# Pooled attention with a mixture-of-depths block: v loaded by parity of heads, keys outermost, and a new order of all operations

## The chip, the cores and the metric

The kernel runs on one core of a Trainium2 chip. The metric is the device time of one execution in microseconds, as the median of several runs. TensorE, VectorE, ScalarE, GpSimd and SyncE run side by side, each its own list of instructions in order; SyncE (SP) issues nearly all transfers, and a core's transfers are carried by 16 DMA engines.

## The reference

q, k and v have the shape (8, 8, 576, 64): batches, heads, positions, width, all float32. k and v are averaged over windows of 8 positions, so each head has 72 pooled keys.

```python
k_p = k.reshape(B, H, Sp, pool, D).mean(axis=3)
v_p = v.reshape(B, H, Sp, pool, D).mean(axis=3)
scores = scale * np.matmul(q, k_p.transpose(0, 1, 3, 2))
attn = softmax(scores)                       # over the 72 pooled keys
x = (attn @ v_p).transpose(0, 2, 1, 3).reshape(B, S, 512)
scores = np.einsum('bsd,d->bs', x, w_gate)   # one number for each row
top_idx = the 128 rows of the batch with the highest score
h = np.maximum(x[top_idx] @ w1, 0.0); ye = h @ w2      # 512 -> 1024 -> 512
out = x;  out[top_idx] = x[top_idx] + sigmoid(scores[top_idx]) * ye
```

## The kernel before

The eight batches go through one pipeline. For each batch `front` declares: fold k over its windows (`pool_k`, L413 and L414), transpose and finish it (`k_trans`, L419 to L428), transpose q in two halves (`q_trans`, L435), scores in two halves on TensorE (L450, L456) with the exponentials on ScalarE (L467), fold v (`pool_v`, L479 to L511), centre its gate column (`centre`), five chunks of attention (`attend`, L550 and L557, division L575 and L579, a store of the rows to `out`), and `rank`, which finds the 128 best rows, gathers them by an indirect DMA and computes their gate. Batches 0 to 3 then go through `dense` one by one (up L731, down L740, scatter L715). Batches 4 and 5, and 6 and 7, go through `pair`, which replaces the eight block products of two batches by seven (`seven`, L824 and L841).

The 72 keys of a head are split into 64 (K0) and 8 left over (K1). The tile VR holds v for one batch, 128 partitions by 5 blocks of 512 numbers (one window of 8 positions by 64 wide, 2 KB). Partitions 0 to 63 belong to even heads, 64 to 127 to odd ones; block 1 + m has the 64 keys of the head pair m, block 0 the leftover keys of all four heads of that parity on 32 partitions. `load_v2` fills the large blocks and `load_v1` the leftover one. There are two tiles VR, one for even and one for odd batches, and only one tile KR for k. KD is the part of the pooled keys that multiplies the leftover scores, masked by `block`; `diag` is the mask that places leftover values of the right head into VP. Both masks come from the number of the partition, by small integer instructions in `opening` (L325 to L330).

Nothing is scheduled when the program is built: every operation is added to a `Plan` with a number, and `ORDER`, a list of all 832 numbers written out in the kernel, is the order in which they are emitted, and so the order within each engine and within SP's queue. `BANKS` gives the PSUM bank of each product that may choose. Operations `heat` (L307) and `fill` (L313) are products of zeros that keep TensorE running. All loads of a batch and all stores are issued by SP from one line (L291), in that order; an issue that has to wait for a buffer or a result holds up all issues behind it.

Of the kernel before, what the change touches and what calls it, by code (L numbers as in the profile page):

```python
# [11 lines left out]
OP = mybir.AluOpType  # L12
# [129 lines left out]
def direct_path(ctx, tc, q, k, v, moe_w_gate, moe_w1, moe_w2, moe_capacity, out, flag):  # L142
# [64 lines left out]
    KD = sb("kd", [128, 2, 2, NP, K1], n=2)  # L207
# [32 lines left out]
    code = sb("code", [128, 2])  # L240
# [57 lines left out]
    def opening():  # L298
# [22 lines left out]
        def grid():  # L321
            for x in VP:
                nc.vector.memset(x[:, 0 : 1 + NP, D], float(POOLW))
            nc.vector.tensor_scalar(ident, ident, 0.0, None, op0=OP.is_equal)
            nc.vector.tensor_scalar(ints[:, 1:2], ints[:, 0:1], 5, None, op0=OP.arith_shift_right)  # L325
            nc.vector.tensor_scalar(ints[:, 2:3], ints[:, 0:1], 3, None, op0=OP.arith_shift_right)
            nc.vector.tensor_scalar(ints[:, 2:3], ints[:, 2:3], 2 * NP - 1, None, op0=OP.bitwise_and)
            nc.vector.tensor_copy(code, ints[:, 1:3])
            nc.vector.tensor_scalar(block, block, code[:, 0:1], None, op0=OP.is_equal)
            nc.vector.tensor_scalar(diag, diag, code[:, 1:2], None, op0=OP.is_equal)  # L330
            nc.vector.memset(heavy[:, 0:NP], float(POOLW))
            nc.vector.tensor_scalar(heavy[:, NP : 3 * NP], diag, float(POOLW), None, op0=OP.mult)
# [54 lines left out]
    def load_v1(b):  # L387
        i = b % 2
        for p in range(2):
            load(VR[i][64 * p : 64 * p + 32, 0], bass.AP(tensor=v.tensor, offset=v.offset + b * H * S * D + p * S * D + K0 * POOLW * D,  # L390
                 ap=[[2 * S * D, NP], [POOLW * D, K1], [1, POOLW * D]]), (), [("VQ", i, p)])

    def load_v2(b):
        i = b % 2
        for m in range(NP):
            load(VR[i][:, 1 + m], bass.AP(tensor=v.tensor, offset=v.offset + b * H * S * D + 2 * m * S * D,
                 ap=[[S * D, 2], [POOLW * D, K0], [1, POOLW * D]]), (), [("VR", i, m)])

    def load_gate():
        w = moe_w_gate  # L400
        for p in range(2):
            load(WG[64 * p : 64 * p + 64, 1 : 1 + NP], bass.AP(tensor=w.tensor, offset=w.offset + p * D, ap=[[0, 64], [2 * D, NP], [1, D]]), (), [("WG", p, 0)])
            load(WG[64 * p : 64 * p + 32, 0], bass.AP(tensor=w.tensor, offset=w.offset + p * D, ap=[[2 * D, NP], [0, K1], [1, D]]), (), [("WG", p, 1)])
# [13 lines left out]
    def k_trans(b):  # L417
# [7 lines left out]
        def two():  # L425
            y = KT[b % 2].rearrange("p j s m -> p (j s) m")
            nc.vector.tensor_tensor(out=y, in0=one_, in1=two_, op=OP.add)
            nc.vector.tensor_tensor(out=KD[b % 2].rearrange("p j s i m -> p (j s) i m"),  # L428
                                    in0=y[:, :, K0:SP].rearrange("p n (one m) -> p n one m", one=1).to_broadcast([128, 4, NP, K1]),
                                    in1=block.rearrange("p (a i b) -> p a i b", a=1, b=1).to_broadcast([128, 4, NP, K1]), op=OP.mult)  # L430
# [41 lines left out]
    def pool_v(b):  # L472
        i = b % 2
        x = VR[i].rearrange("p m (w d) -> p m w d", d=D)
        raw = [("VR", i, m) for m in range(NP)] + [("VQ", i, p) for p in range(2)]
# [274 lines left out]
    def differences():  # L750
        keys = [("VRx", 0)] + [("VR", 0, m) for m in range(NP)]
# [544 lines left out]
```

## Time and profile before

| | us |
|---|---|
| median of 3 runs | 381.98 |
| lowest and highest | 381.77, 384.44 |
| the profiled execution | 382.64 |
| its span from first to last instruction | 380.9 |
| TensorE busy | 238.6 |
| VectorE busy | 171.6 |
| ScalarE busy | 110.8 |
| GpSimd busy | 37.2 |

The profile is one execution. A view of it lists groups of instructions, waits, the chain of work that ended last, or the busy time of each engine in stretches of the span. "PE" is TensorE, "DVE" VectorE, "ACT" ScalarE, "POOL" GpSimd, "SPq" the issuing of transfers by SyncE. [...] "DMA share" is the mean busy share of the 16 DMA engines: 1.0 means that all move data, 0.13 that on the average two of them do.

### The profile page before, as it was taken

What the parts mean: (1) busy time and instruction counts of PE and PEld (TensorE: products, weight loads), DVE (VectorE), ACT (ScalarE), POOL (GpSimd) and SP (SyncE); (2) the same over time, 40 slices, a digit from 0 to 9 for tenths busy, and PEclk for the clock granted to TensorE, in tenths of its full rate; (3) what the DMA queues carried; (4) which work ended last, traced back from release to release, by engine and by line L of the source; (5) the groups of instructions that cost most, each with busy time, mean ns of one, the idle gap of its engine ahead of it and who ended that gap; (6) DMA issues with size and microseconds to landing.
All of it is one profiled execution on the core that took longest, in us unless ns stands there. A gap on an engine that the chain in (4) does not pass through costs nothing.

```text
span 380.9 us, 7492 instructions
## 1 busy us (share of the span) xinstructions
PE 238.6 (63%) x3081; PEld 166.4 (44%) x3081; DVE 171.6 (45%) x380; ACT 110.8 (29%) x372; POOL 37.2 (10%) x96
## 2 busy tenths in 40 slices
PE   5402225919103979803359930977669999999990
PEld 2201113505002648501125820436645677999980
DVE  8104109452007787307045703635173636648751
ACT  1100123605004457302033301362404761641300
POOL 5000000000000040000100300002010431310031
PEclk9955655977855799975588995895859999999996
DMA  5131264712374892115559334534613344200012
GB/s 189 58 111 62 64 195 126 264 48 76 92 241 132 275 364 109 58 55 170 170 153 324 112 123 137 162 137 133 203 40 125 102 139 99 95 29 1 2 55 65
DMA packets 19858, 48.50 MB, mean 127 GB/s; under 512 B 3048, under 2 KB 4072, under 8 KB 18920
## 3 DMA queue, kind: packets, MB, share of 16 engines
q1 hardware_dynamic: 18536, 43.75, 36.1%
q0 software_dynamic: 1280, 4.20, 3.5%
q8 instruction: 26, 0.43, 0.4%
q14 instruction: 16, 0.13, 0.1%
HBM read 36.39 MB, written 11.55 MB: 126 GB/s over the span
## 4 chain that ended last, share of the span: by engine, by line
DMA 41%; PE 28%; SPq 18%; DVE 9%; issue 2%; ACT 0%; POOL 0%; DVEq 0%; POOLq 0%
DMA vr<-in_v_dram 29%; SPq L291 18%; PE pJ L740 5%; DMA kr<-in_k_dram 4%; DMA qr<-in_q_dram 3%; DMA dr<-sc 3%; PE pJ L824 3%; PE pA L550 3%; DVE vr L479 3%; PE pJ L731 2%; PE pA L824 2%; PE pA L841 2%; PE pA L557 2%; PE pJ L841 2%; PE pS L824 1%
## 5 line engine op out<-in xcount | busy, mean ns | idle before, releaser
L550 PE MATMUL pA<-vp,et 64*64 64x66 f32 x1056 | 28.0, 250 | 73.5 <-DVE xs L579 61.2
L479 DVE TENSOR_TENSOR vr<-vr 128x1280 f32<-128x1280 f32 (+1 forms) x16 | 18.5, 1157 | 115.7 <-DMA vr<-in_v_dram 115.3
L550 PEld LDWEIGHTS pA<-vp,et 64*64 64x64 f32 x1056 | 22.5, 156 | 86.1 <-DVE xs L579 64.4
L740 PE MATMUL pJ<-w,ht 128*128 128x512 f32 x64 | 36.7, 708 | 11.7 <-DMA w<-in_moe_w_dram 11.7
L731 PE MATMUL pJ<-xg,w 128*128 128x128 f32 x256 | 35.6, 298 | 0.0
L731 PEld LDWEIGHTS pJ<-xg,w 128*128 128x128 f32 x256 | 33.5, 211 | 4.4 <-issue 3.1
L450 PE MATMUL pS<-qt,kt 32*64 32x320 f32 (+1 forms) x512 | 20.7, 433 | 22.0 <-DVE qt L435 22.0
L664 ACT ACTIVATE cmp<-sr,sc 128x640 bf16<-128x640 f32 (+3 forms) x40 | 32.5, 812 | 3.7 <-DMA sr<-dr 3.1
L570 ACT ACTIVATE za<-pA,eps 128x8 f32<-128x8 f32 (+1 forms) x36 | 9.6, 266 | 76.2 <-PE pA L557 74.9
L500 ACT COPY vp<-vp 32x66 f32<-32x66 f32 x16 | 3.9, 245 | 84.0 <-DVE vp L495 83.9
L467 ACT ACTIVATE et<-pS 128x512 f32<-128x512 f32 (+1 forms) x40 | 21.9, 559 | 16.8 <-PE pS L456 16.7
L557 PE MATMUL pA<-vp,ed 64*64 64x264 f32 (+1 forms) x288 | 25.9, 422 | 0.3 <-issue 0.3
L740 PEld LDWEIGHTS pJ<-w,ht 128*128 128x128 f32 x64 | 13.3, 228 | 26.9 <-issue 13.9
L579 DVE TENSOR_TENSOR xs<-pA,rz 128x512 f32<-128x512 f32 (+1 forms) x34 | 21.9, 644 | 6.0 <-DVE rz L575 2.6
L450 PEld LDWEIGHTS pS<-qt,kt 32*64 32x64 f32 x512 | 9.8, 136 | 31.3 <-DVE qt L435 23.2
L435 DVE STREAM_TRANSPOSE qt<-qr 128x1024 f32<-128x1024 f32 (+1 forms) x16 | 21.9, 1369 | 0.9 <-DMA qr<-in_q_dram 0.8
L715 POOL DMA_INDIRECT out_dram<-y,ix x8 | 9.0, 1126 | 105.0 <-DVE rz L575 42.0
L413 DVE TENSOR_TENSOR kr<-kr 128x1152 f32<-128x1152 f32 (+1 forms) x10 | 11.1, 1110 | 14.4 <-DMA kr<-in_k_dram 14.4
L575 DVE RECIPROCAL rz<-za 128x8 f32<-128x8 f32 (+1 forms) x40 | 7.4, 185 | 19.3 <-ACT za L570 19.2
L686 POOL TENSOR_SCALAR ix<-tg 128x1 int32<-128x1 f32 x8 | 2.4, 294 | 129.5 <-DVE tg L682 129.4
L313 PE MATMUL pJ<-zero 128*128 128x256 f32 x32 | 12.8, 520 | 3.4 <-DVE zero L304 3.4
L456 PE MATMUL pS<-qt,kd 128*32 128x128 f32 (+1 forms) x256 | 12.7, 318 | 0.0
(200 smaller groups left out, 386.2 us busy)
## 6 DMA issues: line engine op xcount, KB each, us to landing
vr<-in_v_dram SPq DMA_DIRECT2D x32, 256.0 KB
out_dram<-xs SPq DMA_DIRECT2D x32, 256.0 KB
kr<-in_k_dram SPq DMA_DIRECT2D x7, 1152.0 KB
qr<-in_q_dram SPq DMA_DIRECT2D x8, 640.0 KB
qr<-in_q_dram SPq DMA_DIRECT2D x8, 512.0 KB
w<-in_moe_w_dram SPq DMA_DIRECT2D x4, 1024.0 KB
sr<-dr SPq DMA_DIRECT2D x5, 320.0 KB
kr<-in_k_dram SPq DMA_DIRECT2D x3, 384.0 KB
```

Source lines behind the costliest of these rows:

```text
L291: i = engine(eng).dma_start(out=dst, in_=src)
L435: nc.vector.transpose(out=QT[b % 2][h].rearrange("p j s (t g) -> p t (j s) g", g=G), in_=QR[b % 2][h].rearrange("p t (j s g) -> p t (j s) ...
L450: nc.tensor.matmul(pS[64 * s : 64 * s + 64, i, 0:n], KT[b % 2][p, j, s, 0:K0], q[p, j, s, 0:n], start=(j == 0), stop=(j == 1))
L467: nc.scalar.activation(o.rearrange("p n (g t) -> p n g t", g=G), pS[:, 0:m, y : y + w].rearrange("p n (t g) -> p n g t", g=G), AF.Exp, sca ...
L479: nc.vector.tensor_tensor(out=o, in0=u, in1=w, op=OP.add)
L550: nc.tensor.matmul(o[s][64 * w : 64 * w + 64, E * y : E * y + E], et[p, m, 64 * u : 64 * u + 64], VP[i][p, 1 + m, :], start=(y == 0), stop ...
L557: nc.tensor.matmul(o[s][64 * w : 64 * w + 64, 0 : n * E], ed[p, u : u + 64], VP[i][p, f : f + n, :], start=False, stop=True)
L579: nc.vector.tensor_tensor(out=XS[i][c].rearrange("p (m s d) -> p s m d", s=2, d=D)[:, k], in0=o[:, :, :, 0:D], in1=RZ[i][:, c, 0:nz].rearr ...
L664: nc.scalar.activation(cmp[0:n, 0:m], SR[r][0:n, 0:m], AF.Sign, bias=SC[i][0:n, c : c + 1], scale=-1.0, accum_out=RK[0:n, b, c])
L731: nc.tensor.matmul(acc[:, cap * f : cap * f + cap], w1[g][:, d, 128 * f : 128 * f + 128], XG[i][:, d, :], start=(d == 0), stop=(d == DB - 1))
L740: nc.tensor.matmul(job(ds)[0:cap, :], HT[i][f // 4][:, f % 4, :], w2[f // 4][:, f % 4, :], start=(f == 0), stop=(f == FB - 1))
L824: nc.tensor.matmul(bank[:, cap * f : cap * f + cap], b[:, d, 128 * f : 128 * f + 128], a[:, d, :], start=d == 0, stop=d == 1)
```

## The change

`load_v2` issues two transfers for a batch instead of four. Before, one transfer took a pair of heads: head, then key, then the 512 numbers of a window, to 128 partitions. After, one takes the heads of one parity: key, then pair, then the 512 numbers, to 64 partitions and four blocks of each. `load_v1` still issues two, but its leftover keys come ordered by key, then pair, instead of pair, then key. The leftover rows of the gate, KD, and the masks follow that order: the mask number of a partition is now its pair plus four times a bit of its 32-block, which takes five small instructions in the opening instead of three. As a batch has two operations fewer, the plan has 816 operations, and `ORDER` and `BANKS` are new.

```diff
 ORDER = [int(x) for x in """
-35 30 28 27 29 36 0 32 2 33 37 50 51 21 7 38 52 4 14 39 53 34 40 41 43 54 47 55 1 44 42 67 56 68 124 45 122 49
...
+2 10 28 35 34 27 4 26 36 49 30 31 29 48 37 32 50 0 38 39 44 41 42 47 45 46 1 43 40 51 121 119 19 8 7 22 21 52
...
-    KD = sb("kd", [128, 2, 2, NP, K1], n=2)
+    KD = sb("kd", [128, 2, 2, K1, NP], n=2)
...
-            nc.vector.tensor_scalar(ints[:, 2:3], ints[:, 0:1], 3, None, op0=OP.arith_shift_right)
-            nc.vector.tensor_scalar(ints[:, 2:3], ints[:, 2:3], 2 * NP - 1, None, op0=OP.bitwise_and)
-            nc.vector.tensor_copy(code, ints[:, 1:3])
+            nc.vector.tensor_scalar(ints[:, 2:3], ints[:, 0:1], NP - 1, None, op0=OP.bitwise_and)
+            nc.vector.tensor_scalar(ints[:, 3:4], ints[:, 1:2], 1, None, op0=OP.bitwise_and)
+            nc.vector.tensor_copy(code, ints[:, 1:4])
+            nc.vector.scalar_tensor_tensor(code[:, 1:2], code[:, 2:3], float(NP), code[:, 1:2], op0=OP.mult, op1=OP.add)
...
             load(VR[i][64 * p : 64 * p + 32, 0], bass.AP(tensor=v.tensor, offset=v.offset + b * H * S * D + p * S * D + K0 * POOLW * D,
-                 ap=[[2 * S * D, NP], [POOLW * D, K1], [1, POOLW * D]]), (), [("VQ", i, p)])
+                 ap=[[POOLW * D, K1], [2 * S * D, NP], [1, POOLW * D]]), (), [("VQ", i, p)])
 
     def load_v2(b):
         i = b % 2
-        for m in range(NP):
-            load(VR[i][:, 1 + m], bass.AP(tensor=v.tensor, offset=v.offset + b * H * S * D + 2 * m * S * D,
-                 ap=[[S * D, 2], [POOLW * D, K0], [1, POOLW * D]]), (), [("VR", i, m)])
+        for p in range(2):
+            load(VR[i][64 * p : 64 * p + 64, 1 : 1 + NP], bass.AP(tensor=v.tensor, offset=v.offset + b * H * S * D + p * S * D,
+                 ap=[[POOLW * D, K0], [2 * S * D, NP], [1, POOLW * D]]), (), [("VR", i, p)])
...
-            load(WG[64 * p : 64 * p + 32, 0], bass.AP(tensor=w.tensor, offset=w.offset + p * D, ap=[[2 * D, NP], [0, K1], [1, D]]), (), [("WG", p, 1)])
+            load(WG[64 * p : 64 * p + 32, 0], bass.AP(tensor=w.tensor, offset=w.offset + p * D, ap=[[0, K1], [2 * D, NP], [1, D]]), (), [("WG", p, 1)])
...
-            nc.vector.tensor_tensor(out=KD[b % 2].rearrange("p j s i m -> p (j s) i m"),
-                                    in0=y[:, :, K0:SP].rearrange("p n (one m) -> p n one m", one=1).to_broadcast([128, 4, NP, K1]),
-                                    in1=block.rearrange("p (a i b) -> p a i b", a=1, b=1).to_broadcast([128, 4, NP, K1]), op=OP.mult)
+            nc.vector.tensor_tensor(out=KD[b % 2].rearrange("p j s m i -> p (j s) m i"),
+                                    in0=y[:, :, K0:SP].rearrange("p n (m one) -> p n m one", one=1).to_broadcast([128, 4, K1, NP]),
+                                    in1=block.rearrange("p (a b i) -> p a b i", a=1, b=1).to_broadcast([128, 4, K1, NP]), op=OP.mult)
...
-        raw = [("VR", i, m) for m in range(NP)] + [("VQ", i, p) for p in range(2)]
+        raw = [("VR", i, p) for p in range(2)] + [("VQ", i, p) for p in range(2)]
```

## Rows read from the trace of the kernel before

**Rows 1.** The page: busy time of the engines, then the shares of the last chain by line.

```profile
PE 238.6 (63%) x3081; PEld 166.4 (44%) x3081; DVE 171.6 (45%) x380; ACT 110.8 (29%) x372; POOL 37.2 (10%) x96
...
DMA vr<-in_v_dram 29%; SPq L291 18%; PE pJ L740 5%; DMA kr<-in_k_dram 4%; DMA qr<-in_q_dram 3%; DMA dr<-sc 3%; PE pJ L824 3%; PE pA L550 3%; DVE vr L479 3%; PE pJ L731 2%; PE pA L824 2%; PE pA L841 2%; PE pA L557 2%; PE pJ L841 2%; PE pS L824 1%
```

**Rows 2.** VectorE's waits: releaser, then total us, times, longest us.

```profile
DVE vr L479 <- DMA vr<-in_v_dram: 115.3, 7, 24.8
...
DVE kr L413 <- DMA kr<-in_k_dram: 14.4, 2, 8.5
DVE vr L491 <- DMA wg<-in_moe_w_gate_dram: 9.1, 1, 9.1
```

**Rows 3.** Chain that ended last, the longest of six pieces of v: start us, us.

```profile
92.18 21.11 DMA vr<-in_v_dram
```

**Rows 4.** DMA view of 0 to 30 us in 40 slices of 0.75 us.

```profile
DMA  0077999783111111111112112111114899211111
GB/s 0 0 106 303 397 369 380 198 360 142 52 49 55 49 49 55 49 49 55 49 49 98 55 63 79 55 49 49 49 49 93 168 358 319 83 49 49 49 52 57
```

**Rows 5.** Stretches: us, busy us (instructions) of each engine, clock, DMA share, GB/s.

```profile
8.50:15.00 6.50, 4.38 (x57) 2.33 (x56) 2.08 (x4) 1.25 (x3) 0.00 (x0) 1.00 0.13 51
134.00:143.00 9.00, 6.68 (x161) 3.80 (x159) 7.81 (x15) 4.70 (x16) 3.90 (x7) 1.00 1.04 365
```

**Rows 6.** The page's transfers by group: issuer, count, KB each.

```profile
vr<-in_v_dram SPq DMA_DIRECT2D x32, 256.0 KB
```

**Rows 7.** Stretches of 4 to 275 us, columns as in rows 5.

```profile
0.00:274.90 274.90, 146.59 (x2164) 92.62 (x2164) 111.70 (x241) 75.35 (x274) 18.73 (x65) 0.75 0.47 150
13.00:274.90 261.90, 138.80 (x2107) 88.50 (x2105) 102.67 (x196) 73.33 (x272) 13.87 (x33) 0.74 0.47 150
113.40:155.90 42.50, 33.23 (x584) 23.25 (x585) 33.85 (x65) 22.83 (x87) 4.10 (x7) 0.82 0.60 204
274.90:300.00 25.10, 20.49 (x322) 11.83 (x322) 16.16 (x36) 8.18 (x30) 2.66 (x4) 0.80 0.23 70
300.00:366.00 66.00, 66.00 (x570) 57.48 (x570) 38.53 (x83) 27.29 (x69) 13.45 (x26) 1.00 0.24 70
124.00:128.00 4.00, 4.00 (x46) 2.80 (x49) 3.61 (x5) 0.75 (x6) 0.00 (x0) 0.50 0.79 266
```

**Rows 8.** SP in order of time: start, us, what it issues.

```profile
75.50 8.82 SPq L291 DMA_DIRECT2D vr<-in_v_dram  x3
...
178.19 0.54 SPq L291 DMA_DIRECT2D vr<-in_v_dram  x1
```

**Rows 9.** A group of instructions by line: busy us, mean ns of one | idle before.

```profile
L428 DVE TENSOR_TENSOR kd<-kt,block 128x128 f32<-128x128 f32 x8 | 2.3, 292 | 0.3
```

**Rows 10.** TensorE at full clock: up and down, then one chunk of attend in the chain.

```profile
302.07 4.63 PE L731 MATMUL pJ<-xg,w 128*128 128x128 f32 x40
...
311.94 3.70 PE L740 MATMUL pJ<-w,ht 128*128 128x512 f32 x8
...
306.69 0.63 PE pA L550 x32
307.32 0.45 PE pA L557 x8
```

**Rows 11.** VectorE in order of time: first q transpose, first folds of batches 0 and 7.

```profile
9.41 1.24 DVE L435 STREAM_TRANSPOSE qt<-qr 128x1024 f32<-128x1024 f32 x1
...
31.22 2.35 DVE L479 TENSOR_TENSOR vr<-vr 128x1280 f32<-128x1280 f32 x2 [20.57 <-DMA vr<-in_v_dram]
...
274.89 2.35 DVE L479 TENSOR_TENSOR vr<-vr 128x1280 f32<-128x1280 f32 x2 [10.50 <-DMA vr<-in_v_dram]
```

**Rows 12.** SP's waits up to 275 us: releaser, total us, times, longest us.

```profile
SPq L291 <- DVE xs L579: 15.2, 3, 9.1
SPq L291 <- DVE rz L575: 13.4, 5, 5.2
...
SPq L291 <- DMA dr<-sc: 10.9, 1, 10.9
```

More of the change, by code (lines that the diff above doesn't have):

```diff
@@ L239, in direct_path @@
     ints = sb("ints", [128, 6], I32)
-    code = sb("code", [128, 2])
+    code = sb("code", [128, 3])
     block = sb("block", [128, NP])
@@ L750, in differences @@
     def differences():
-        keys = [("VRx", 0)] + [("VR", 0, m) for m in range(NP)]
+        keys = [("VRx", 0)] + [("VR", 0, p) for p in range(2)]
         t1 = [(part(VR[0], 0, 2, 512), keys), (part(VR[0], 1024, 2, 512), keys), (part(QR[0][0], 0, 2, 512), [("QR", 0, 0)]),
```

63 rows, old and new, of tables (BANKS, ORDER) are left out of this document.

## The prediction

> **What bounds the kernel now.** I read the page first: no engine is busy for more than 63% of the span, yet transfers of v and SP's issuing hold nearly half of the chain that ended last (29% and 18%) [rows 1]. So the time is waiting, and the list of waits says whose: VectorE stands 115.3 us, in seven waits, before the first fold of v (L479) until a load of v has landed; 14.4 us more go on k and 9.1 us on the gate [rows 2]. In the chain six pieces "DMA vr<-in_v_dram" follow one another, the longest 21.11 us [rows 3].
>
> The DMA view of the first 30 us shows why they are so long. While k and the first half of q are in flight the core moves 303 to 397 GB/s; from about 8 us on, with only v in flight, the share is 0.1 and the rate 49 to 55 GB/s [rows 4]. Measured over 8.5 to 15 us it is a share of 0.13 at 51 GB/s; where everything flows (134 to 143 us) it is 1.04 at 365 GB/s [rows 5]. 0.13 of 16 engines is two engines, at some 25 GB/s each. The source of each large load of v has an outer dimension of 2 (the two heads of a pair), those of k and q one of 128. A load of 256 KB [rows 6] over two engines takes 262 KB / 51 GB/s = 5.1 us, four of them 20.6 us: the pieces of the chain.
>
> That is throughput, not latency. 32 such loads hold two engines for 32 x 5.1 = 164 us. Up to 274.9 us, where the last v is folded, the share is 0.47, so 129 us of all sixteen [rows 7]; 164 x 2/16 = 20.5 of it is v's, and the other loads and stores put about 109 us on every engine. The two that carry v thus have 109 + 164 = 273 us to do in 274.9 us. They are the bound of the front of the kernel; k, q, weights and stores have a share on the same two and queue behind v, and SP's issues block: three issues of v take 8.82 us, against 0.54 us for one that meets no queue [rows 8]. After 300 us TensorE is the bound, 66.0 of 66.0 us busy [rows 7].
>
> **The change, part by part.** *Large v loads:* four of 256 KB become two of 512 KB, outer dimension 64 keys on both sides, 2 KB pieces as before. No row has a load of that shape, so its rate lies between two engines (51 GB/s) and sixteen (365 GB/s) [rows 5]; the nearest row is that of loads with an outer dimension of 128, and I take sixteen: 1.05 MB in 2.9 us instead of 20.6 us. [...]
>
> *Small v loads, gate loads:* 64 KB and 8 KB, outer dimension 4 becomes 8. They are a twentieth of v's bytes; a gain of up to 1 us each, hidden behind the large ones, which land later. I count zero; uncovered it is 0 to 1 us per batch. The 9.1 us wait for the gate goes, since what it queued behind is gone.
>
> *SP:* 16 issues fewer, 16 x 0.54 = 9 us of SP's time [rows 8], counted at nothing: SP is ahead once its issues no longer block. Per batch this leaves no wait that was not there; the order decides which transfer queues behind a waiting one (rival C).
>
> *Key-first layout:* the product that fills kd (L428) still writes 128 x 128 elements, 0.29 us [rows 9]; were the inner broadcast costlier, it could double, 8 x 0.3 = 2.4 us; I take 0, as elements and operands are the same. The setup gets two more VectorE instructions on one column; each no longer than that product, 0 to 0.6 us in an opening that waits for loads, taken as 0.
>
> *New order:* what counts is where it puts work against the folds. In its SP list k, half of q, half of v and the gate come first, then the rest of q and v. In its VectorE list both transposes of q stand before the first fold. And ahead of the last batch's first fold TensorE now has four groups "up" and five "down" of batch 2 and two chunks of attend that came behind it before. At full clock these are 4 x 0.46, 5 x 0.46 and 2 x 1.08 us [rows 10], with a pick 6.5 us.
>
> **The sum.** Opening: by the shapes 3.6 MB stand up to the end of v(0), at 365 GB/s [rows 5] 10 us, after the 2 us until data flow [rows 4]. VectorE has the first q transposed at 10.7 us and needs 1.5 us for the second, which is a quarter larger [rows 11]. So the first fold comes at 13 us instead of 31.2 us [rows 11].
>
> Front: now the first folds of batch 0 and batch 7 are 274.89 - 31.22 = 243.7 us apart, 34.8 us per batch [rows 11]. What a batch costs with v at hand is seen from 113.4 to 155.9 us, from the first fold of batch 2 to the point where VectorE waits for batch 4: two batches in 42.5 us, VectorE 33.85 us or 80% busy, granted clock 0.82 [rows 7]. Seven times 21.25 us is 149 us. The other way, VectorE's work: 111.7 us before 274.9 us [rows 7], some 4 us that the order moves ahead (an estimate: a difference of weights, a one-hot and divisions), less 10.5 us before the first fold (9.0 us up to 13 us today [rows 7] and the second transpose), is 105 us; at 80% 132 us. I take the middle, 141 us: the stretch began with a cold TensorE (clock 0.50 up to 128 us [rows 7]), which a front without long waits doesn't have, but it needed a DMA share of only 0.60. The new front needs 129 us of share in 154 us, 0.84, which the engines reach where they are fed [rows 5]; TensorE's 146.6 us there [rows 7] fit even at today's clock. So VectorE with its hand-overs is what is late next.
>
> Tail: 380.9 - 274.9 = 106 us, less the 6.5 us moved ahead = 99.5 us.
>
> 13 + 141 + 99.5 = 253.5 us of span; the profiled execution's 382.64 us stands 1.7 us over its span of 380.9 us and 0.7 us over the median: **255 us**.
>
> **Rivals.** *A, the forecast:* v spread over sixteen engines, the front at VectorE's pace: 246 to 263 us (132 and 149 us for the front), with some 4 us to either side 242 to 267 us.
>
> *B, v lands at half rate and the transfers stay the bound.* Each new load writes 64 partitions instead of 128. If such a load moves at half of 365 GB/s while it holds the queue, v keeps all engines 5.8 us per batch instead of 2.9, and the front's demand rises from 129 to 152 us; at a share of 0.9 that takes 169 us up to the last fold, at 0.84 it takes 181 us, where the sum has 13 + 141 = 154 us: 255 + 15 to 255 + 27, 270 to 282 us. For it: no row shows such a load. Against it: it decides only if the share stays under 152/154, and the order can spread the load. [...]
>
> *C, other waits of SP's in-order queue come on the path.* In front of 275 us SP waits also for divisions (xs 15.2, rz 13.4 us) and for dr (10.9 us) [rows 12]. Whatever load stands behind such a wait is late too. If these 40 us stay and nothing hides them: 255 + 40 = 295 us; half of it 275. Against it: the waits are long because the divisions wait for v themselves.
>
> *D, better than the stretch:* VectorE at 90% in the front, 117 us: 231 us; with the tail's cold part (0.80 up to 300 us [rows 7]) warm as well some 3 us less. So 231 to 242 us. Against it: the best long stretch has 80%.
>
> *E, no spread, slower.* If the shape does not set the number of engines, v stays at 51 GB/s. Then the new VectorE list hurts: the folds of batch 1 stand ahead of the shift that batch 0's attend needs, so two batches of v, 41 us of two engines, come before the first attend, as now, and every later load is issued in an order made for quick v. Today's 382 us, plus up to one load of 20 us: 385 to 402 us. It decides only from where a batch of v takes as long as now, 20 us; at 10 us the front is already shorter than 34.8 us per batch. The same kind of transfer with outer dimensions of 128 and of 2 side by side [rows 4] speaks against it.
>
> **Chances.** A 0.52, B 0.17, C 0.14, D 0.12, E 0.03, and 0.02 that gains and losses cancel. The range takes A and B whole, half of D and the lower two thirds of C: 237 to 288 us, some 0.84. A, B, C and D are all faster by far more than the 1% that a measurement of this kernel can tell from no change: faster 0.95, same 0.02, slower 0.03.
>
> **What would show it.** Right: the waits of L479 for v fall from 115 to under 25 us; a stretch in which v flows alone has a share above 0.5; first folds of batches 19 to 22 us apart, the first at 13 us; the last 100 us look as now. B: share high but under 200 GB/s while v flows. C: SP waits for xs, rz or dr as long as now, with VectorE idle behind k or q. E: share 0.13 again. My number is wrong if the front is bound by something of which today's trace shows no queue, such as ScalarE's exponentials or accumulators that come free late; then VectorE's share in the front stays under 65% and the time comes out above 285 us.

## The result: 256.25 us, and the profile after

The changed kernel takes 256.25 us (median of 4 runs, 254.21 to 256.51), beside 382.53 us for the kernel before on the same chip: a ratio of 0.668, 95% interval 0.664 to 0.673. The prediction was 255 us with a range of 237 to 288. The profiled execution has a span of 254.3 us. Executions over 1.5% longer than the fastest of their kernel (269.85 beside 259.12 us in `old_order`) are left out of the ratios here and below, while each median, lowest and highest is that of all executions.

The page of after, in the order of [rows 1] and [rows 6]: busy times, shares of the chain by engine, the queue of all loads and stores, the large loads of v.

```profile
PE 223.3 (88%) x3081; PEld 155.1 (61%) x3081; DVE 171.9 (68%) x381; ACT 110.9 (44%) x372; POOL 37.0 (15%) x96
...
q1 hardware_dynamic: 18800, 43.75, 57.7%
...
PE 32%; POOL 0%; DVE 0%; issue 0%; DVEq 0%
...
vr<-in_v_dram SPq DMA_DIRECT2D x16, 512.0 KB
```

TensorE, at 63% before, is at 88%. Its 3081 products take 223.3 us instead of 238.6, at a mean granted clock of 0.93 instead of 0.80 (the clock granted to TensorE, as a share of its full clock). The chain that ended last, which this view follows back over 32% of the span, is TensorE's alone; before, transfers of v and SP's issues held nearly half of the span in it [rows 1]. VectorE's work is the same to 0.3 us, as the change meant.

VectorE's longest waits in after (releaser, total us, times, longest us):

```profile
DVE rz L575 <- ACT za L570: 20.4, 19, 3.1
DVE m L527 <- PE pJ L522: 9.8, 4, 4.4
DVE vr L479 <- DMA vr<-in_v_dram: 4.4, 2, 2.6
DVE kr L413 <- DMA kr<-in_k_dram: 3.6, 1, 3.6
```

The wait for v, 115.3 us in [rows 2], is 4.4 us; the 9.1 us for the gate row are gone. First in the list stand the hand-overs of the division, 20.4 us in 19 short pieces.

The DMA view of 0 to 30 us in slices of 0.75 us, as in [rows 4]:

```profile
DMA  0068998779999988995899999999999989899999
GB/s 0 0 94 299 397 336 255 199 284 396 243 201 198 153 137 168 302 355 212 87 339 199 189 172 180 186 210 202 167 235 240 270 329 418 351 381 389 407 427 401
```

Where [rows 4] had a 1 under v, there is now an 8 or 9: all engines are busy. But look at the second line: beneath those nines the rate is 137 to 243 GB/s for most of 7.5 to 23 us (the slices from 9.75 to 12 us also hold the gate's 256-byte pieces: 418 of their 528 packets are under 512 bytes), and mostly 350 to 427 GB/s after that. The engines were busy twice as long per byte while v flowed: 186 GB/s at a share of 1.06 in the first stretch below, against 365 GB/s at 1.04 in [rows 5]. A share near 1 alone would have hidden this.

Stretches of after, columns as in [rows 5]: one with v in flight, then the front in two halves, then the dense tail.

```profile
16.00:20.00 4.00, 3.78 (x50) 1.69 (x42) 2.13 (x3) 1.25 (x3) 0.00 (x0) 0.50 1.06 186
...
0.00:90.00 90.00, 66.38 (x1032) 36.36 (x1033) 58.84 (x138) 37.86 (x150) 8.33 (x44) 0.81 0.89 260
90.00:165.00 75.00, 75.00 (x1235) 50.85 (x1242) 59.87 (x119) 40.39 (x135) 11.35 (x23) 1.00 0.83 249
165.00:247.00 82.00, 81.85 (x824) 67.91 (x808) 52.15 (x115) 32.65 (x89) 16.38 (x28) 1.00 0.24 75
```

Up to 90 us TensorE has idle time (66.38 of 90 us busy, 22.1 of them with the products of zeros, `heat` and `fill`) and the DMA share is 0.89. From 90 to 165 us TensorE is busy without a gap (75.00 of 75.00 us) at a clock of 1.00, and none of its products there is one of zeros.

The first folds of batches 0 and 1, and of batch 7, from VectorE in order of time (compare [rows 11]):

```profile
18.30 2.35 DVE L479 TENSOR_TENSOR vr<-vr 128x1280 f32<-128x1280 f32 x2 [1.83 <-DMA vr<-in_v_dram]
24.82 2.35 DVE L479 TENSOR_TENSOR vr<-vr 128x1280 f32<-128x1280 f32 x2 [2.59 <-DMA vr<-in_v_dram]
...
159.50 1.49 DVE L479 TENSOR_TENSOR vr<-vr 128x1280 f32<-128x1280 f32 x1
```

So the three terms of the sum measured: opening 18.3 us (predicted 13), front 159.5 - 18.3 = 141.2 us (141), tail 254.3 - 159.5 = 94.8 us (99.5). The sum is right because its errors cancel, so that it came within 2 us is luck; the experiments below show that the middle term is right for a reason other than the one given.

### The profile page after: what moved, and what is told of

It is laid out like the page before. It is cut to its first block, busy times and chain, and to the rows that moved or that the text cites. A ratio compares the mean times of both kernels' runs of the same rounds, so it can differ in the third digit from the quotient of the medians.

```text
span 254.3 us, 7464 instructions
## 1 busy us (share of the span) xinstructions
PE 223.3 (88%) x3081; PEld 155.1 (61%) x3081; DVE 171.9 (68%) x381; ACT 110.9 (44%) x372; POOL 37.0 (15%) x96
## 5 line engine op out<-in xcount | busy, mean ns | idle before, releaser
L550 PE MATMUL pA<-vp,et 64*64 64x66 f32 x1024 | 24.8, 228 | 13.3 <-issue 8.1
L550 PEld LDWEIGHTS pA<-vp,et 64*64 64x64 f32 x1024 | 19.6, 135 | 25.6 <-issue 14.4
L731 PE MATMUL pJ<-xg,w 128*128 128x128 f32 x256 | 32.2, 280 | 0.1
L731 PEld LDWEIGHTS pJ<-xg,w 128*128 128x128 f32 x256 | 29.7, 192 | 4.1 <-issue 3.2
L740 PE MATMUL pJ<-w,ht 128*128 128x512 f32 x64 | 31.1, 605 | 0.0
L450 PE MATMUL pS<-qt,kt 32*64 32x320 f32 (+1 forms) x512 | 24.7, 488 | 6.8 <-DVE qt L435 5.2
L557 PE MATMUL pA<-vp,ed 64*64 64x264 f32 (+1 forms) x288 | 22.7, 377 | 0.0
L575 DVE RECIPROCAL rz<-za 128x8 f32<-128x8 f32 (+1 forms) x40 | 7.6, 191 | 21.6 <-ACT za L570 20.4
L631 POOL CAST aux<-sc 128x5 bf16<-128x5 f32 x8 | 4.8, 600 | 82.1 <-DVE sc L626 71.1
L740 PEld LDWEIGHTS pJ<-w,ht 128*128 128x128 f32 x64 | 10.8, 190 | 8.9 <-issue 8.0
L715 POOL DMA_INDIRECT out_dram<-y,ix x8 | 8.0, 999 | 46.4 <-DVE y L855 32.2
L306 PE MATMUL pS<-zero 128*128 128x512 f32 x16 | 11.6, 853 | 1.4 <-DVE zero L303 1.4
```

The lines of the kernel that those rows point to most:

```text
L450: nc.tensor.matmul(pS[64 * s : 64 * s + 64, i, 0:n], KT[b % 2][p, j, s, 0:K0], q[p, j, s, 0:n], start=(j == 0), stop=(j == 1))
L550: nc.tensor.matmul(o[s][64 * w : 64 * w + 64, E * y : E * y + E], et[p, m, 64 * u : 64 * u + 64], VP[i][p, 1 + m, :], start=(y == 0), stop ...
L557: nc.tensor.matmul(o[s][64 * w : 64 * w + 64, 0 : n * E], ed[p, u : u + 64], VP[i][p, f : f + n, :], start=False, stop=True)
L731: nc.tensor.matmul(acc[:, cap * f : cap * f + cap], w1[g][:, d, 128 * f : 128 * f + 128], XG[i][:, d, :], start=(d == 0), stop=(d == DB - 1))
L740: nc.tensor.matmul(job(ds)[0:cap, :], HT[i][f // 4][:, f % 4, :], w2[f // 4][:, f % 4, :], start=(f == 0), stop=(f == FB - 1))
```

## The experiments

Each ratio is to runs of the kernel before on the same chip, measured beside it, with its 95% interval. Spans and stretches come from one profiled execution, which can lie some us off the median.

**Theory before the runs.** The spread over sixteen engines is what gained (A), and what was left in the new kernel is partly the half rate that rival B named. Rivals: the order gained; VectorE, or TensorE, is the whole of the new bound.

### old_order and old_loads: the change in its two parts

`old_order` has the new loads, with the numbers of the old list (each parity's load at the place of the first and the third old load of its batch). `old_loads` has the new list with the four old loads and the old key order.

```diff
 # old_order
-2 10 28 35 34 27 4 26 36 49 30 31 29 48 37 32 50 0 38 39 44 41 42 47 45 46 1 43 40 51 121 119 19 8 7 22 21 52
+(the list of the kernel before)
 # old_loads
-        for p in range(2):
+        for m in range(NP):
-                 ap=[[POOLW * D, K0], [2 * S * D, NP], [1, POOLW * D]]), (), [("VR", i, p)])
+                 ap=[[S * D, 2], [POOLW * D, K0], [1, POOLW * D]]), (), [("VR", i, m)])
```

> The changed kernel with the order and banks of the kernel before (each parity's load stands where the first and the third of the four loads of its batch stood). Theory 1, the number of engines that carry v made the gain: the front is free of the two full engines whatever the order, 262 to 285 us, VectorE waits under 25 us for v. Theory 2, the new order made the gain: 330 us or more, with new waits of VectorE in place of those for v.

Measured: 262.26 us (259.12 to 269.85), ratio 0.677, 0.672 to 0.682.

> The kernel before (four loads of 256 KB with an outer dimension of 2) with the new order and banks; the first two loads of a batch stand where the first parity's load stands, the other two where the second's stands. Theory 1: v is again carried by two engines for 164 us beside 109 us of other transfers, so 375 to 400 us, waits for v above 100 us. Theory 2: 256 to 300 us.

Measured: 372.46 us (372.13 to 372.78), ratio 0.973, 0.966 to 0.980. That is 2.5 us under the range of theory 1. VectorE's waits before the first fold of v are put down to v for 51.1 us, not for the 100 us expected; another 50.7 us of them are put down to q's loads and to stores:

```profile
DVE vr L488 <- DMA vr<-in_v_dram: 51.1, 4, 15.4
DVE vr L488 <- DMA qr<-in_q_dram: 36.9, 3, 21.2
...
DVE vr L488 <- DMA out_dram<-xs: 13.8, 1, 13.8
```

A stretch of its opening:

```profile
20.00:24.00 4.00, 0.00 (x0) 0.00 (x0) 1.07 (x1) 0.00 (x0) 0.00 (x0) 0.54 0.13 50
```

The loads alone are worth 116 to 123 of the 126 us. The order is worth 10 us where v is slow (382 to 372 us); where v is quick it is 3 us by the ratios (0.677 to 0.668), whose intervals just overlap, so that gain is not clear of noise. The old loads have their share of 0.13 in either list, at 50 GB/s here and 51 GB/s in [rows 5].

### split_62_2 and split_57_7: is it the outer dimension?

The kernel after, with the same bytes, rows and partitions, but the 64 keys of each large load cut into 62 and 2, or 57 and 7. The theory that the two runs test: a load is carried by as many engines as the largest number up to 16 that divides its outer dimension, which is 2 for 62 and 3 for 57.

```diff
-            load(VR[i][64 * p : 64 * p + 64, 1 : 1 + NP], ... ap=[[POOLW * D, K0], [2 * S * D, NP], [1, POOLW * D]]), ...
+                for a, z in ((0, 62), (62, 64)):        # split_57_7: ((0, 57), (57, 64))
+                    nc.sync.dma_start(out=VR[i][64 * p + a : 64 * p + z, 1 : 1 + NP], ... ap=[[POOLW * D, z - a], [2 * S * D, NP], [1, POOLW * D]])
```

> The changed kernel, same order, same layout, same bytes to the same places; only each large load of 64 keys is cut into one of 62 keys and one of 2. 62 has 2 as its largest divisor up to 16 and 64 has 16. Theory 1 in its sharp form (the outer dimension of the transfer sets how many engines carry it): v alone in flight shows a DMA share of 0.13 and some 51 GB/s again, and the time is 375 to 400 us. Rival (it is the layout by key, the larger transfer or the new order that helps): 254 to 262 us and a share near 1.

Measured: 394.48 us (393.26 to 395.70), ratio 1.030, 1.022 to 1.038.

```profile
8.00:12.00 4.00, 0.73 (x4) 0.31 (x2) 3.78 (x25) 0.20 (x1) 0.00 (x0) 1.00 0.13 34
20.00:24.00 4.00, 0.00 (x0) 0.00 (x0) 0.00 (x0) 0.00 (x0) 0.00 (x0) 0.50 0.13 40
```

> The kernel after, with the 64 keys of each large load of v cut into 57 and 7: the outer dimensions are 57 = 3 x 19 and 7, and neither has a divisor between 4 and 16 except 7 itself. Theory (the number of engines is the largest number up to 16 that divides the outer dimension): 0.93 MB of a batch go over three engines; at the 20 to 25 GB/s an engine that the traces show for two, 60 to 75 GB/s and 12 to 16 us per batch, so the eight batches put 100 to 125 us on those three engines beside 109 us of other transfers; a stretch with v alone has a DMA share near 0.19, and the time lies between the kernel after (256) and the run with 62 and 2 (394): 300 to 340 us. Rival 1 (any odd or uneven number falls back to two engines or one): share 0.13 or 0.06 and 385 us or more. Rival 2 (only very small outer dimensions are slow and 62 was slow for another reason): 256 to 270 us.

Measured: 316.93 us (316.28 to 317.59), ratio 0.828, 0.823 to 0.833.

```profile
20.00:24.00 4.00, 2.00 (x32) 0.98 (x32) 1.51 (x1) 0.00 (x0) 0.00 (x0) 0.59 0.22 78
...
21.00:23.00 2.00, 1.00 (x16) 0.67 (x24) 0.85 (x1) 0.00 (x0) 0.00 (x0) 0.50 0.19 73
```

```profile
DVE vr L482 <- DMA vr<-in_v_dram: 52.3, 7, 14.5
```

Taking two of 64 keys into a load of their own costs 138 us and undoes the whole change, and more: a share of 0.13 is that of two engines (2/16). With 57 keys the share is 0.19, that of three engines (3/16), at 73 GB/s, and the wait for v is 52.3 us, between the 4.4 us of after and the 115.3 us of [rows 2]. Two, three and sixteen engines give 394, 317 and 256 us. Both edits also make four large loads of a batch out of two; `narrow_64` below has four as well and is no slower than after, so their number is not the cause. The shares agree with the theory at these three points (0.13 with 62 keys, 0.19 with 57, 1.06 with the 64 of after); no other cut of the keys was run. What stays open is why two engines moved only 34 to 40 GB/s with 62 keys, where the old loads had 49 to 55 on two [rows 4] and 57 keys 73 GB/s on three, some 24 on each by division.

### wide_128 and narrow_64: is it the 64 partitions?

`wide_128` keeps the outer dimension of 64 keys, but puts the head of the pair second, so that a load of 256 KB fills 128 partitions; the rows of v come to other partitions than the scores expect, while all work is the same. `narrow_64` also has four loads of 256 KB and 64 keys, each into 64 partitions.

```diff
 # wide_128, for each pair m
+    out=VR[i][:, 1 + m], ... ap=[[POOLW * D, K0], [S * D, 2], [1, POOLW * D]]
 # narrow_64, for each parity p and half n
+    out=VR[i][64 * p : 64 * p + 64, 1 + 2 * n : 3 + 2 * n], ... ap=[[POOLW * D, K0], [2 * S * D, 2], [1, POOLW * D]]
```

> The changed kernel, same order; each large load writes a head pair to all 128 partitions (four of 256 KB a batch) with the keys as outer dimension 64 and the head of the pair second. Key and parity are interleaved over the partitions, so the attention is computed with v's rows exchanged: the same work on other numbers. Theory 3 (a load that writes 64 partitions moves at about half rate, which cost the opening some 5 us and is hidden later): more than 300 GB/s where v flows in the opening, first fold at 13 to 14 us instead of 18.3, 248 to 252 us in all. If the half rate held back the front as a whole: under 245 us. If there is no half rate: 254 to 258 us and the first fold at 18 us.

Measured: 242.23 us (239.07 to 244.24), ratio 0.627, 0.622 to 0.632; first fold at 16.2 us. The theory's 248 to 252 us was missed: the gain is not that of the opening alone.

> The kernel after, with each of its 512 KB loads of v cut by pairs into two of 256 KB: four loads per batch of the size and outer dimension (64 keys) of the run wide_128, but each writes 64 partitions where wide_128 wrote 128. It tells the number of partitions apart from the number and size of the loads. Theory (the 64 partitions halve the rate): nothing changes against the kernel after, 252 to 259 us, and where v flows alone the rate stays at 150 to 225 GB/s with a DMA share near 1. Rival (what wide_128 gained came from smaller loads or from shorter source streams): 240 to 246 us, over 300 GB/s in the first 20 us, first fold near 16 us.

Measured: 252.61 us (249.65 to 253.54), ratio 0.655, 0.650 to 0.660; first fold at 19.2 us. Four microseconds of each in which v flows alone, `wide_128` first:

```profile
14.00:18.00 4.00, 3.65 (x58) 1.78 (x43) 3.26 (x3) 1.26 (x3) 0.00 (x0) 0.58 0.98 324
```

```profile
16.00:20.00 4.00, 3.78 (x48) 1.58 (x38) 2.30 (x2) 1.25 (x3) 0.00 (x0) 0.50 1.07 194
```

Same size, number and outer dimension: 324 GB/s into 128 partitions, 194 into 64, both with the engines busy nearly all the time (shares of 0.98 and 1.07). So in this pair the partitions set the rate, and they cost about 10 us in the time (0.655 to 0.627). Taken apart by first folds, as the sum was, the opening is 16.2 instead of 19.2 us and the front 130.3 instead of 137.0 us, 9.8 us together:

```profile
16.21 2.35 DVE L482 TENSOR_TENSOR vr<-vr 128x1280 f32<-128x1280 f32 x2 [0.22 <-DMA vr<-in_v_dram]
...
146.46 1.49 DVE L482 TENSOR_TENSOR vr<-vr 128x1280 f32<-128x1280 f32 x1
```

```profile
19.21 2.35 DVE L482 TENSOR_TENSOR vr<-vr 128x1280 f32<-128x1280 f32 x2 [1.59 <-DMA vr<-in_v_dram]
...
156.23 1.49 DVE L482 TENSOR_TENSOR vr<-vr 128x1280 f32<-128x1280 f32 x1
```

What in the hardware lowers the rate into 64 partitions, no run shows. Smaller loads themselves may have gained some 1 to 2% on the kernel after (0.668 to 0.655, measured apart); what of that is the chip was not told apart.

### run_128 and run_128_gate: 128 partitions, with each key where the scores expect it

Both parities can lie in one run of 128 consecutive windows: leave over keys 0 to 7 of even heads and keys 64 to 71 of odd ones. The 64 last keys of an even head and the 64 first ones of the odd head behind it then follow each other in memory, and a load has an outer dimension of 128 into 128 partitions. Two such loads of 512 KB make a batch; the leftover loads and the scores take the keys from their new places, and `kd` is made in two instructions. `run_128_gate` moves the gate loads behind the second half of q and the first large load of v.

```diff
-        for p in range(2):
-            load(VR[i][64 * p : 64 * p + 64, 1 : 1 + NP], ... ap=[[POOLW * D, K0], [2 * S * D, NP], [1, POOLW * D]]), ...
+        for n in range(2):
+            load(VR[i][:, 1 + 2 * n : 3 + 2 * n], ... offset=... + 4 * n * S * D + K1 * POOLW * D,
+                 ap=[[POOLW * D, 2 * K0], [2 * S * D, 2], [1, POOLW * D]]), ...
...
```

> The changed kernel with the same order, but with other keys as the leftover ones: keys 0 to 7 for even heads, 64 to 71 for odd heads. Then the 64 keys of a pair's even head and the 64 of its odd head are 128 consecutive windows in memory, and one load with an outer dimension of 128 fills all 128 partitions: two loads of 512 KB a batch. The product that writes kd becomes two of half the size. Theory 3 (half rate into 64 partitions costs the changed kernel about 14 us): 240 to 245 us with the right result. If what made the run with interleaved partitions quick was something else (its four smaller loads): 252 to 257 us.

Measured: 238.37 us (236.50 to 241.52), ratio 0.622, 0.618 to 0.626: 18 us under the kernel after, and some 2 us under the range expected. One stretch has v alone, the next is that of after:

```profile
13.00:17.00 4.00, 3.20 (x49) 1.73 (x50) 3.94 (x4) 0.11 (x1) 0.00 (x0) 0.50 0.84 288
16.00:20.00 4.00, 3.78 (x50) 1.74 (x42) 3.69 (x6) 2.10 (x7) 0.00 (x0) 0.50 1.02 395
...
0.00:90.00 90.00, 76.64 (x1283) 46.80 (x1287) 70.55 (x169) 46.31 (x178) 12.62 (x51) 0.89 0.86 303
15.16:144.00 128.84, 122.13 (x2183) 78.92 (x2167) 105.33 (x212) 72.27 (x267) 13.82 (x34) 0.93 0.82 284
```

```profile
15.16 2.35 DVE L480 TENSOR_TENSOR vr<-vr 128x1280 f32<-128x1280 f32 x2
...
144.00 1.49 DVE L480 TENSOR_TENSOR vr<-vr 128x1280 f32<-128x1280 f32 x1
```

With v alone the loads move 288 GB/s at a share of 0.84 (by division, an estimate, 343 GB/s for engines that are always busy), against 186 at 1.06 in after. (The 395 GB/s of 16 to 20 us are not v's: k's large load is in flight there with it: 93 of the 480 packets are of 8 KB or more, where v's pieces are 2 KB.) Taken apart as the sum was: opening 15.2 us, front 144.0 - 15.2 = 128.8 us, tail 238.9 - 144.0 = 94.9 us. Against after that is -3.1, -12.4 and +0.1 us: 15.5 us of span, most of it in the front, where TensorE by 90 us was busy 76.64 us with 1283 products instead of 66.38 us with 1032. `narrow_64` and `wide_128`, which differ only in the partitions that a load writes and the rows that it takes, show 9.8 us of that kind; that the other 5.7 us are the half rate too is not shown, as `run_128` also changes the outer dimension, the leftover keys and `kd`.

> As the run with 128 consecutive windows, and the four gate loads, whose pieces are 256 bytes and which now keep q's second half and half of v(0) waiting in the opening, are issued behind them. If the opening is held up by the gate loads: q's second transpose and the first fold 2 to 3 us sooner, 237 to 242 us. If TensorE's list decides from the start: the same as without the move, within 1 us.

Measured: 237.26 us (235.80 to 238.78), ratio 0.619, 0.615 to 0.622; first fold at 15.04 us. It can't be told from `run_128`: the gate loads are not what keeps the opening over 13 us.

### two_queues: can two queues serve both halves at once?

```diff
+            ..., [("VR", i, p)], eng="ACT" if p and b < 2 else "SP")
```

> The kernel after, with the odd-parity large load of v of batches 0 and 1 issued by ScalarE instead of SP, so that the loads into partitions 0 to 63 and into 64 to 127 stand in two queues. It tells whether the half rate of a 64-partition load is a limit of one queue at a time, which two queues together lift, or of something both share. Theory (each half is limited by its own partitions, and side by side the two halves run at the full rate): over 300 GB/s while both flow, first fold at 15 to 16 us instead of 18.3, and 252 to 255 us. Rival (two halves still follow one another, since one set of engines takes the packets of both): rate stays at 150 to 225 GB/s, first fold at 18 us or later, 255 to 260 us, with ScalarE delayed by its issues.

Measured: 254.03 us (250.53 to 255.66); first fold at 18.1 us. From 18 to 20 us, the rate and the two queues (packets, MB, share of 16 engines):

```profile
DMA packets 203, 0.39 MB, mean 196 GB/s; under 512 B 12, under 2 KB 12, under 8 KB 203
...
q10 hardware_dynamic: 169, 0.32, 87.5%
q1 hardware_dynamic: 34, 0.07, 17.9%
```

ScalarE's queue (q10) holds the engines for 87.5% while SP's gets 17.9%, and the sum is still 196 GB/s. The halves mostly follow one another (q10 and q1 have 84.5% and 10.5% from 14 to 18 us, 0.8% and 107.0% from 20 to 24 us), and the second queue brought nothing: rate and first fold are those of the rival, and the time, though in the theory's range, is that of after within noise. ScalarE issued both odd halves from 12.4 us on, when the first even half was already on its way, and most of what flows from 18 to 20 us is one half, so this run tells nothing of two halves that start together.

### half_up, less_vector and run_half: which engine is the bound now?

`half_up` leaves out half of the products "up" of batches 0 to 3 (TensorE, half of L731's 32.2 us). `less_vector` leaves out 16 us of folds of k and v on VectorE. `run_half` is `run_128` with the edit of `half_up`.

```diff
 # half_up, run_half
-                    for d in range(DB):
+                    for d in range(DB // 2):
...
 # less_vector
-                e.tensor_tensor(out=x[:, a:z, 0:2], in0=x[:, a:z, 0:2], in1=x[:, a:z, 2:4], op=OP.add)
+                if b == 0:
+                    e.tensor_tensor(out=x[:, a:z, 0:2], in0=x[:, a:z, 0:2], in1=x[:, a:z, 2:4], op=OP.add)
...
-            fold(x[:, :, 0:2], x[:, :, 0:2], x[:, :, 2:4])
```

> The changed kernel without half of TensorE's work in the up products of batches 0 to 3 (the sum over 512 runs over 256 only: 128 of 256 products of L731, 128 x 0.126 = 16 us), nothing taken from VectorE. Theory 4: in the changed kernel TensorE is the bound from about 90 us on (75.0 of 75.0 us busy from 90 to 165 us), so 12 to 16 us go: 240 to 244 us. Prediction's own view (VectorE with its hand-overs is what is late next): 253 to 257 us.

Measured: 247.22 us (246.02 to 253.75), ratio 0.646, 0.640 to 0.651: 9 of the 16 us, between the two ranges.

> The changed kernel without some of VectorE's work, nothing taken from TensorE: the first fold of k for batches 1 to 7 (7 x 1.35 us) and the second of the three folds of v (8 x 0.82 us) are left out, 16 us in all, so that k and v are averaged over part of their window. Theory 4 (TensorE binds after 90 us): only what VectorE holds up before 90 us comes back, 250 to 256 us. If VectorE is the bound: 240 to 244 us.

Measured: 251.87 us (249.69 to 254.62), ratio 0.656, 0.652 to 0.661: 4.4 of the 16 us. TensorE is as full from 90 us on as it was:

```profile
90.00:165.00 75.00, 75.00 (x1253) 49.66 (x1254) 52.71 (x113) 39.47 (x134) 8.99 (x19) 1.00 0.79 233
```

On the kernel after, 16 us less of TensorE count twice as much as 16 us less of VectorE, and neither counts in full.

> The kernel run_128 with half of the up products of batches 0 to 3 left out, as in half_up: 16 us of TensorE less, everything else as in run_128; h is computed from half of its inputs, so this run's numbers are not the reference's. Theory (in the kernel after, TensorE binds only from about 90 us on, and before that the half-rate loads of v do; with these quick, TensorE binds nearly everywhere): the 16 us count more than the 9 they counted on the kernel after, 224 to 228 us, 11 to 15 under run_128. Rival 1 (the two limits always share the time, whatever the loads do): 229 to 231 us, 8 to 9 under it. Rival 2 (VectorE takes over at once): 232 us or more.

Measured: 233.90 us (232.28 to 234.71), ratio 0.611, 0.608 to 0.614: only some 4 of the 16 us. The theory of that run fell, and the time is in the range of its rival 2.

```profile
0.00:90.00 90.00, 74.20 (x1276) 44.33 (x1277) 73.19 (x174) 49.23 (x188) 12.66 (x51) 0.94 0.91 317
90.00:165.00 75.00, 71.00 (x1300) 43.47 (x1299) 57.74 (x122) 43.41 (x144) 12.94 (x30) 1.00 0.66 214
```

TensorE's waits from 90 to 165 us:

```profile
PE pA L551 <- DVE xs L580: 3.9, 6, 1.5
```

With less to do, TensorE has gaps again behind 90 us (71.00 of 75 us), and 3.9 of these 4.0 us are waits for VectorE's divisions; VectorE is busy 73.19 of the first 90 us, 81%. I had reasoned from `run_128`'s 91% TensorE that TensorE would pay in full. That VectorE is what then takes over is read from these waits, not tested: no run takes VectorE's work out of `run_128`, and the transfers, at a share of 0.91 up to 90 us, are a rival.

## Why the prediction was right, point by point

**The bound of before, and the cure.** Right, and shown: v held two engines by the outer dimension of its loads, and the cut into 62 and 2 alone brings the old time back (394 us beside 382, at a share of 0.13 in both). The share and the rate of [rows 5] carried this. That all loads of v hold the same two engines, on which the 273 us rest, no view shows.

**Rate of the new loads.** The step took 365 GB/s "from the nearest row", that of loads with an outer dimension of 128. This is the step that failed: 186 GB/s with v alone, at a share of 1.06. The nearest row was near in the outer dimension and far in the number of partitions. Rival B had named the half rate, and its sign, "share high but under 200 GB/s", was there to see; the chance of 0.17 stood for its price in time, not for its being there. B's half of 365 GB/s was an assumption that no run showed when it was made; 186 GB/s (after) and 194 (`narrow_64`) were measured in its place.

**B's price.** It was given as 15 to 27 us. `narrow_64` against `wide_128` measures some 10 us for the partitions alone, `run_128` against after 15.5 us of span and 18 us of median with its other changes. So the price was at its lower end or too high, and it was added to a sum that was already too long by about as much. Its demand of 152 us was also 3 us low: 109 us of other transfers and 8 x 5.8 us of v are 155 us.

**Opening.** 18.3 instead of 13 us, mis-sized by 5.3 us. Of these some 3 us are the half rate (18.3 to 15.2 us in `run_128`, 19.2 to 16.2 us in the matched pair). The other 2.2 us remain there too: in its stretch of 12 to 16 us the engines move 252 GB/s at a share of 0.80, where the sum had 365 throughout.

**Front.** 141.2 us against 141, yet not for the reason given. Its work was right to the decimal: 105 us of VectorE were predicted, and the front of after has 104.96. But the rate, "the middle" of 132 and 149 us, was for a front with v at hand, and such a front is that of `run_128`: 128.8 us, VectorE at 82% (105.33 of 128.84 us). So the way by 80% of VectorE gave the right time (132), the stretch in which TensorE had a clock of 0.82 did not; but TensorE is busy 95% of that front (122.13 us), so it is not shown that VectorE sets it. In after 12.4 us come on top, some 6.8 of them by the half rate (the matched pair), which lowers VectorE to 74%. The mean distance of the first folds, 141.2 / 7 = 20.2 us, lies in the 19 to 22 that were named; the single distances run from 6.5 us (above) to 27.2 us (51.97 less 24.82), as the two tiles VR let batch 1 follow batch 0 at once. The front and the tail of after as stretches:

```profile
18.30:159.50 141.20, 124.48 (x2150) 78.91 (x2151) 104.96 (x204) 71.11 (x264) 13.80 (x34) 0.90 0.86 258
159.50:254.30 94.80, 87.41 (x866) 70.48 (x866) 56.61 (x130) 37.05 (x103) 18.37 (x30) 0.98 0.27 85
```

**"VectorE with its hand-overs is what is late next."** Half right. In after it is mostly transfers until about 90 us (a share of 0.89; with the quicker loads of `run_128` TensorE is busy 76.64 us there instead of 66.38), then TensorE, 75.00 of 75.00 us, though `half_up` gets back only 9 of 16 us of it. "TensorE's 146.6 us fit even at today's clock" compared a sum with a sum; the work is not spread evenly, as the dense products come late. VectorE is what TensorE waits for behind 90 us where v is quick and TensorE is eased (`run_half`).

**Tail.** 94.8 us instead of 99.5: TensorE is busy 87.41 us with 866 products at a clock of 0.98 in it, where that part of before had 91.99 us with 917 at 0.92. D's "3 us less" for a quicker clock in the tail had been left out of the forecast; how much is the clock and how much the work that the order moved ahead was not told apart.

```profile
274.90:380.90 106.00, 91.99 (x917) 73.78 (x917) 59.93 (x140) 35.46 (x99) 18.51 (x31) 0.92 0.23 68
```

**So the sum.** Against `run_128`, whose loads of v move 288 GB/s where after's move 186, the terms 13 + 141 + 99.5 stand beside 15.2 + 128.8 + 94.9 = 238.9 us: 15 us too long, and `run_128` is in the place of rival D (231 to 242). The step from `run_128` to after, of which the half rate is shown to be some 10 us and was counted at nothing, brought 15.5 us back. 255 against 256 is a right bound, a right size of the main effect, and two errors that happen to be of one size: the range was earned, the last 2 us were luck.

**Order and the rest.** The order was counted only as work moved; taken alone it gives 10 us where v is slow, and some 3 us, not clear of noise, where v is quick. Rival E said that the new list hurts where v is slow: `old_loads` is 2.7% faster than before, so that was wrong. Of rival C, SP's waits for divisions fell (xs 22.6 to 13.1 us over the whole span, rz gone) and those for dr from 14.1 to 3.3 us; the waits for `sc` rose from 4.4 to 25.8 us in their place and stayed hidden, since VectorE waits 4.4 us for v and 3.6 us for k in all. kd is still 292 ns, and the setup's two more instructions take 155 and 160 ns: nothing, as counted.

## What to carry to other kernels

Read a transfer's share and its rate together: here a share of 0.13 (at 51 GB/s) with v alone in flight came from an outer dimension that spread a load over two engines, and a share near 1 at half of the usual rate (1.06 at 186 GB/s, beside 1.04 at 365) from a destination of half of the partitions. The cure for the first brought in the second, and choosing which rows are left over so that both halves become one run of 128 (`run_128`, 238 us, 288 GB/s with v alone) cured both. When a sum comes out right, take its terms apart on the chip before trusting the steps, and look at what each engine does from stretch to stretch, as a sum of busy time that "fits" can still leave an engine full for the second half.

## What the hardware showed that was not expected

Two of 64 rows moved into a load of their own made the kernel 138 us slower (256 to 394 us, a share of 0.13), where a cut into two loads of 64 keys each (`narrow_64`) made it no slower (252.61 beside 256.25 us). With 64-partition loads the engines are shown as busy (share 1.06) at 186 GB/s, so what the partitions cost shows up as work in the busy share. And two engines moved 34 to 40 GB/s with the cut into 62 and 2, against 49 to 55 in the old loads (and 73 on three engines with the cut into 57 and 7); the cause of that was not found.
